# Sigmoid attention with a SiLU MLP behind it: the order of values and first products in the paired h stages, and the last set's stores

## The chip, the cores and the metric

The kernel runs on one core of one Trainium2 chip. The metric is device time in microseconds of one execution, the median of three runs. PE is the matrix engine, DVE, ACT and POOL are the vector, scalar and GpSimd engines, SP is the engine that issues most of the stores and the DMA transposes. Each engine works through its own instructions in order and waits on semaphores of the others.

## The reference

Eight batches, 12 heads, 448 positions, head size 64. Attention without a softmax, then an MLP over the 8 x 448 = 3584 rows of 768:

```python
scores = scale * np.matmul(q, k.transpose(0, 1, 3, 2)) - np.log(S)
attn = 1.0 / (1.0 + np.exp(-scores))
attn_out = np.matmul(attn, v)
...
x = attn_out.transpose(0, 2, 1, 3).reshape(B * S, H * D)
h = x @ w_in                          # 768 -> 2048
g = h * (1.0 / (1.0 + np.exp(-h)))
out = g @ w_out                       # 2048 -> 768
```

Inputs and output are float32.

## The kernel before

**Attention.** Heads are taken in quads of four; a batch has three quads (NQ), the kernel 24. `scores` (L218) makes one of a quad's seven rounds (NCH): eight matmuls of the 64*64 form into two PSUM banks (psc), then one activation on ACT into an attnT tile. `values` (L240) multiplies attnT by v: 28 matmuls of the 64*64 form, four for each round, into two banks (pav); its argument `end` stops it after so many rounds, and a later call goes on from there. After the last round DVE scales the two banks into xT (L267).

**h.** Batches 0 and 1 get their h by plain products. Batches 2 and 3, 4 and 5, 6 and 7 are taken in pairs, in three "paired h stages" (`h_pair`): a seven-product scheme over halves of w_in (wi, SI) and sums of x (tx, made on DVE by `x_sums`, L357). Each product is three matmuls of the 128*128 form with 448 columns (L378). Its first product m1 (bank pa) reads the first half of the even batch's x alone and is copied by ACT (L394); m2 adds to the same bank and SiLU on ACT writes g (gTr, L372); m5, m6, m7, m3 and m4 (banks pd, pb, pc) need the sums. The sums of the first two quads are made earlier; those of the last quad, which is the last to get its values, are made inside the stage:

```python
def last_values():
    values(g)
    after_values(g)
    for _ in x_sums(m + 1, NQ - 1, NQ):
        pass
    nc.gpsimd.tensor_copy(gate, tx[m + 1, 4][:1, NQ - 1, :1])
...
order = [(m1, 0), (m1, 1), (last_values,), (m1, 2)]
for i in range(3):
    order += [(m2, i), (silu11, i)]
order += [(m5, 0), (m6, 0), (m7, 0), (h22, 0), (m1, 3)]
```

`after_values` issues the next load of v from POOL. In the kernel before, `values(g, NCH - 1)` (L796) ahead of `h_pair` does six of the last quad's seven rounds, and `last_values` the seventh.

**PSUM banks.** Around each stage the eight banks change hands. `banks_for_h` (L78) makes a ring of them: first the two banks of the pair longest idle, then the two single banks (of the last po products), then the other pairs. `one_bank` takes them in that order, round and round.

**Output.** `sets(m)` goes through the rows of g in pairs of 128-row blocks, and `out_set` (L487) makes one pair's output by a seven-product scheme over halves of w_out; each product (po, L504) is eight matmuls of the 128*128 form with 384 columns, 0.163 us each. DVE adds them up into two output tiles osb (c11 and c12 are the halves of the first, c21 and c22 of the second). The stores are issued by SP and, at the very end, by ACT, 64 rows each (`store`, L497). In the last set of all, L514 is a copy on ACT, and the first block is stored in two halves: the left one behind L518, the right one behind L539.

The order of the whole is fixed by the program: scores and values of the next two batches are woven into the products of `sets`, then come the last products of `sets`, the paired stage, and the next `sets`. The last `sets` (from 326 us) has no attention beside it.

Of the kernel before, what the change touches and what calls it, by code (L numbers as in the profile page):

```python
# [17 lines left out]
def kernel(  # L18
# [9 lines left out]
    nc = tc.nc  # L28
# [6 lines left out]
    NCH = S // HP  # L35
# [28 lines left out]
    def banks_for_attention(doubles):  # L64
        psum.close()
        banks.clear()
        bufs_of.update(double=doubles, single=NBANK - 2 * doubles)
        for name, bufs in bufs_of.items():
            taken[name] = 0
            new_pool(name, bufs)  # L70
# [18 lines left out]
    def one_bank(name):  # L89
        if "any" in banks:  # L90
            ring.append(ring.pop(0))
            return banks["any"].tile([P, 512], F32, tag=f"any{ring[-1]}", name=name)
        taken["single"] += 1
        return banks["single"].tile([P, 512], F32, tag="single", name=name)

    def two_banks(name):
        taken["double"] += 1
        return banks["double"].tile([P, 2, 512], F32, tag="double", name=name)
# [141 lines left out]
    def values(g, end=NCH):  # L240
        b, iq = divmod(g, NQ)
        if b not in xT:
            assert b < 2 or b - 2 in h_done
            xT[b] = p2.tile([P, NPAIR, S], F16, tag="xT", name="xT")
        pav, done_rounds = part_of.pop(g, None) or (None, 0)
        if pav is None and bufs_of["double"] > 2 and "any" not in banks:
            both = two_banks("pav")
            pav = [both[:, half] for half in range(2)]
        elif pav is None:
            pav = [one_bank("pav") for _ in range(2)]  # L250
        for ch in range(done_rounds, end):
            at = attnT.pop((g, ch))
            for half in range(2):
                own = slice(half * HP, (half + 1) * HP)
                for j in range(2):
                    nc.tensor.matmul(  # L256
                        pav[half][j * D : (j + 1) * D, :S],
                        flat["v", g][own, j, ch, :],
                        at[own, j, :],
                        start=(ch == 0),  # L260
                        stop=(ch == NCH - 1),
                    )
        if end < NCH:
            part_of[g] = pav, end
            return
        for half in range(2):
            nc.vector.tensor_scalar_mul(xT[b][:, half * NQ + iq, :], pav[half][:, :S], SX)  # L267
        if iq == NQ - 1:
            ready.add(b)
# [217 lines left out]
    def out_set(a1, rows1, a2, rows2, last=False):  # L487
        lo, hi = slice(0, NHC), slice(NHC, NFC)
        osb = [p3.tile([P, DMODEL], F32, tag="osb", name="osb") for _ in range(2)]
        c11, c12 = (osb[0][:, nh * NO2 : (nh + 1) * NO2] for nh in range(2))  # L490
        c21, c22 = (osb[1][:, nh * NO2 : (nh + 1) * NO2] for nh in range(2))
        m1 = cpool.tile([P, NO2], F32, tag="m1", name="m1")
        sg = [cpool.tile([P, NHC, P], F16, tag=f"S{i}", name=f"S{i}") for i in range(1, 5)]

        def store(rows, o, cols, engines):
            for at, (row, eng) in enumerate(zip(rows, engines)):
                eng.dma_start(row[:, cols], o[at * HP : (at + 1) * HP, cols])  # L497

        left, right, whole = slice(0, NO2), slice(NO2, DMODEL), slice(0, DMODEL)

        def product(a, w):
            po = one_bank("po")
            for fc in range(NHC):
                nc.tensor.matmul(  # L504
                    po[:, :NO2], a[:, fc, :], w[:, fc, :], start=(fc == 0), stop=(fc == NHC - 1)
                )
                if fc < NHC - 1:
                    yield 163
            return po[:, :NO2]

        add, sub = nc.vector.tensor_add, nc.vector.tensor_sub
        add(sg[0], a2[:, lo], a2[:, hi])
        po = yield from product(a1[:, lo], wq[0][0])
        (act_copy if last else nc.vector.tensor_copy)(m1, po)  # L514
        sub(sg[1], sg[0], a1[:, lo])  # L515
        yield 163
        po = yield from product(a1[:, hi], wq[1][0])
        add(c11, po, m1)  # L518
        sub(sg[2], a1[:, lo], a2[:, lo])
        if last:  # L520
            store(rows1, osb[0], left, (nc.sync, nc.sync))
        yield 163
        po = yield from product(sg[1], tw[2])
        add(c12, po, m1)
        sub(sg[3], a1[:, hi], sg[1])
        yield 163
        po = yield from product(sg[2], tw[3])
        add(c22, po, c12)
        yield 163
        po = yield from product(a2[:, hi], tw[4])  # L530
        sub(c21, c22, po)
        yield 163
        po = yield from product(sg[0], tw[1])
        add(c22, po, c22)
        add(c12, po, c12)
        store(rows2, osb[1], whole, (nc.sync, nc.sync))
        yield 163
        po = yield from product(sg[3], wq[1][1])
        add(c12, po, c12)  # L539
        if last:  # L540
            store(rows1, osb[0], right, (nc.sync, nc.scalar))
        else:
            store(rows1, osb[0], whole, (nc.sync, nc.sync))
        yield 163
# [25 lines left out]
    def sets(m):  # L570
        for g in range(0, NCH - 1, 2):
            step = out_set(
                block(m, g), row_blocks(m, g), block(m, g + 1), row_blocks(m, g + 1)
            )
            for i, ns in enumerate(step):
                if m == 0 and g == 0 and i in (10, 14):
                    next(sums)
                if m == 0 and g == 0 and i in (20, 28, 36, 44):
                    next(in_sums)
                yield ns  # L580
        if m % 2 == 1:
            g = NCH - 1
            yield from out_set(
                kept, row_blocks(m - 1, g), block(m, g), row_blocks(m, g), m == B // 2 - 1
            )
# [152 lines left out]
    def burst(n, size=2):  # L738

        new = units[n : n + size]  # L740
        for u in new:
            scores(*u)
        with_values = values_if_any()
        for g, ch in new:
            if ch == NCH - 1:
                waiting.append(g)
                if 9 <= g + 3 < NQB:
                    later.extend(((g + 3, "k"), (g + 3, "q")))
        return with_values
# [15 lines left out]
    for m in range(B // 2 - 1):  # L765
        banks_for_attention(3)
        nc.scalar.activation(warm, bias_s, AF.Sigmoid)
        stream = sets(m)
        for _ in range(FIRST_DENSE):
            next(stream)  # L770

        dense = (3 + m % 2) * 7 * NHC - FIRST_DENSE - ENDING
        sizes = [2, 2, 3]
        costs = sum(SWITCH + TILE * size for size in sizes) * 2 * NQ + VALUES * (2 * NQ - 1)
        total = dense * DENSE + costs
        own = 2 * NQ * (m + 2)
        left, n = 0.0, 2 * NT_B * (m + 1)
        for size in sizes * (2 * NQ):
            left += total * size / (2 * NT_B) - SWITCH - TILE * size - VALUES * burst(n, size)
            n += size  # L780
            rows_if_any(own, nc.vector.tensor_copy)
            count = max(1, round(left / DENSE))
            left -= count * DENSE
            half = count // 2
            for i in range(count):
                next(stream)
                if i == half:
                    rows_if_any(own, nc.vector.tensor_copy)
        assert not sums_of_x
        nc.scalar.activation(warm, bias_s, AF.Silu)  # L790
        for _ in stream:
            pass
        (g,) = waiting
        waiting.clear()
        banks_for_h()
        values(g, NCH - 1)  # L796

        def last_values():
            values(g)
# [5 lines that stand above are left out]
        for i, _ in enumerate(h_pair(m + 1, last_values)):  # L805
            if i % 8 == 7:
                rows_if_any(NQB, nc.gpsimd.tensor_copy)
# [33 lines left out]
```

## Time and profile before

| | |
|---|---|
| median of 3 runs | 369.92 us (369.61 to 370.37) |
| the profiled execution | 369.69 us |
| its span, first to last instruction | 367.7 us |
| granted PE clock over the span | 0.999 of full speed |
| PE busy | 359.5 us (98%) |
| DVE, ACT, POOL busy | 251.9, 249.9, 77.8 us |
| the paired stages begin (values of the last quad) | 122.7, 212.1, 292.9 us |
| the last `sets` begins | 326.4 us |
| last matmul ends, last add ends, span ends | 363.6, 364.1, 367.7 us |

In the profile's rows, L378 is a line of the kernel, "out<-in" names the tiles, "128x448" is partitions by elements, and "xN" is the number of instructions that a row stands for. In the chain of waits a row is: start, duration, engine, tile, line, count. In the time line a row also has, in brackets, how long the engine had been idle and what ended that. In the DMA view a row has the tile, the issuing engine, the number of issues, the size of each, and the median time from issue to landing. Matmuls overlap in PE's pipeline, so a single matmul lasts longer than the distance from its start to the next one's.

### The profile page before, as it was taken

The numbers are of one execution on the slowest core, as the hardware profiler recorded it, in microseconds if no ns is written. First come the engines' busy times: TensorE is split into PE (matmuls) and PEld (weight loads), VectorE is DVE, ScalarE is ACT, GpSimd is POOL, SyncE is SP. The second block draws the span as 40 slices with busy tenths as digits, with TensorE's granted clock in tenths as the row PEclk, the third lists the DMA queues.
The fourth block names the chain that finished last, engine by engine and source line by source line (L and its number), as shares of the span: only waits on it lengthen the run. The fifth ranks groups of instructions, "written<-read, shape, count | busy, mean of one in ns | idle before, by whom it ended". The sixth has DMA issues, their size and how long they took to land. (4 is left out here: it accounts for less than half of the span.)

```text
span 367.7 us, 7596 instructions
## 1 busy us (share of the span) xinstructions
PE 359.5 (98%) x3009; PEld 183.2 (50%) x3009; DVE 251.9 (68%) x458; ACT 249.9 (68%) x339; POOL 77.8 (21%) x116
## 2 busy tenths in 40 slices
PE   7999999999999999999999999999999999999995
PEld 2554445545544555544444545554455545555553
DVE  2565569867657587867665758795756667797763
ACT  5998885479998755687777846679998856640000
POOL 8566521040060172000051047000100000000000
PEclk9999999999999999999999999999999999999999
DMA  8999999989969499007589369912863020003333
GB/s 142 200 202 202 204 204 203 187 116 141 164 100 227 110 128 180 2 0 166 92 165 206 61 128 144 128 15 51 153 111 86 21 69 0 3 0 86 87 86 86
DMA packets 65698, 42.78 MB, mean 116 GB/s; under 512 B 36096, under 2 KB 62208, under 8 KB 65664
## 3 DMA queue, kind: packets, MB, share of 16 engines
q0 software_dynamic: 27072, 22.58, 42.3%
q1 hardware_dynamic: 38240, 19.44, 26.8%
q8 instruction: 23, 0.38, 0.4%
q10 hardware_dynamic: 352, 0.30, 0.2%
q14 instruction: 11, 0.09, 0.1%
HBM read 45.61 MB, written 11.01 MB: 154 GB/s over the span
## 5 line engine op out<-in xcount | busy, mean ns | idle before, releaser
L232 ACT ACTIVATE attnT<-psc,bias_s 128x896 f16<-128x896 f32 x168 | 158.1, 1009 | 21.9 <-PE psc L225 21.6
L504 PEld LDWEIGHTS <-S 128*128 128x128 f16 x448 | 41.3, 98 | 36.5 <-issue 8.1
L225 PE MATMUL psc<-qT,kT 64*64 64x448 f16 x672 | 51.1, 362 | 1.5 <-ACT qT L186 0.6
L267 DVE TENSOR_SCALAR xT<-pav 128x448 f16<-128x448 f32 x48 | 27.7, 620 | 33.2 <-PE pav L256 33.2
L124 POOL DMA_DIRECT2D vf<-in_v_dram x24 | 17.2, 717 | 135.0 <-PE pav L256 120.9
L504 PEld LDWEIGHTS <-gTr 128*128 128x128 f16 x336 | 31.3, 98 | 26.6 <-issue 7.7
L504 PE MATMUL po<-T,S 128*128 128x384 f16 x224 | 42.0, 327 | 0.2 <-DVE S L515 0.2
L504 PE MATMUL po<-w_out_sb,gTr 128*128 128x384 f16 x224 | 41.6, 327 | 0.0
L378 PEld LDWEIGHTS <-w_in_sb 128*128 128x128 f16 x288 | 27.7, 98 | 26.9 <-issue 1.7
L504 PE MATMUL po<-w_out_sb,S 128*128 128x384 f16 x224 | 40.8, 326 | 0.0
L256 PE MATMUL pav<-attnT,vf 64*64 64x448 f16 x672 | 38.9, 350 | 0.5 <-DVE gTr L303 0.4
L288 PE MATMUL ph<-xT,w_in_sb 128*128 128x448 f16 x192 | 38.7, 353 | 0.1
L378 PE MATMUL pa<-xT,w_in_sb 128*128 128x448 f16 x144 | 33.2, 353 | 0.0
L225 PEld LDWEIGHTS <-kT 64*64 64x64 f16 x672 | 17.8, 104 | 28.8 <-issue 22.3
L378 PEld LDWEIGHTS <-SI 128*128 128x128 f16 x216 | 21.1, 98 | 20.0 <-issue 0.5
L256 PEld LDWEIGHTS <-vf 64*64 64x64 f16 x672 | 21.0, 106 | 14.0 <-issue 4.7
L288 PEld LDWEIGHTS <-w_in_sb 128*128 128x128 f16 x192 | 17.8, 98 | 19.1 <-issue 3.7
L394 ACT ACTIVATE part<-pa 128x448 f32<-128x448 f32 x24 | 13.1, 544 | 19.9 <-PE pa L378 19.0
L504 PE MATMUL po<-T,gTr 128*128 128x384 f16 x112 | 22.1, 327 | 0.0
L372 ACT ACTIVATE gTr<-pc 128x448 f16<-128x448 f32 x24 | 13.1, 544 | 12.9 <-DVE pc L388 12.5
L388 DVE TENSOR_TENSOR part<-pb,part 128x448 f32<-128x448 f32 x24 | 14.9, 621 | 8.3 <-ACT part L394 5.0
L186 ACT ACTIVATE m<-po 128x384 f32<-128x384 f32 x1 | 0.5, 491 | 27.7 <-PE po L504 27.7
(75 smaller groups left out, 467.7 us busy)
## 6 DMA issues: line engine op xcount, KB each, us to landing
out_dram<-osb SPq DMA_DIRECT2D x54, 192.0 KB, 3.0
vf<-in_v_dram POOLq DMA_DIRECT2D x24, 224.0 KB, 7.0
kf<-in_k_dram POOLq DMA_DIRECT2D x23, 224.0 KB, 7.7
qf<-in_q_dram POOLq DMA_DIRECT2D x23, 224.0 KB, 7.9
w_in_sb<-in_moe_w_in_dram POOLq DMA_DIRECT2D x16, 192.0 KB, 8.2
w_out_sb<-in_moe_w_out_dram POOLq DMA_DIRECT2D x4, 768.0 KB, 14.9
kT<-kr SPq DMA_TRANSPOSE x18, 4.1
qT<-qr SPq DMA_TRANSPOSE x18, 4.8
```

Source lines behind the costliest of these rows:

```text
L124: nc.gpsimd.dma_start(flat[name, g][:, :, c0:c1].rearrange("p i c d -> p i (c d)"), rows_in(name, g)[:, :, c0 * D : c1 * D],)
L186: nc.scalar.activation(o, i, AF.Copy)
L225: nc.tensor.matmul(psc[own, j, :S], qkT["k", g][rows, ch, own], qkT["q", g][rows, :, own], start=True, stop=True,)
L232: nc.scalar.activation(attnT[g, ch], psc[:, :, :S], AF.Sigmoid, bias=bias_s, scale=QKSCALE)
L256: nc.tensor.matmul(pav[half][j * D : (j + 1) * D, :S], flat["v", g][own, j, ch, :], at[own, j, :], start=(ch == 0), stop=(ch == NCH - 1),)
L267: nc.vector.tensor_scalar_mul(xT[b][:, half * NQ + iq, :], pav[half][:, :S], SX)
L288: nc.tensor.matmul(ph[:, :S], w_in_sb[:, cc, fc * P : (fc + 1) * P], xT[b][:, cc, :], start=(at == 0), stop=(at == NCC - 1),)
L372: nc.scalar.activation(gTr[:, r * NG + i, col + c * S : col + (c + 1) * S], h, AF.Silu, bias=0.0, scale=ISX)
L378: nc.tensor.matmul(to, w[:, n, i * P : (i + 1) * P], x[:, n], start=(start and n == 0), skip_group_check=not start, stop=(n == NQ - 1),)
L388: nc.vector.tensor_add(o, po, x)
L394: nc.scalar.activation(got[i, 1], bank[i, "a"], AF.Copy)
L504: nc.tensor.matmul(po[:, :NO2], a[:, fc, :], w[:, fc, :], start=(fc == 0), stop=(fc == NHC - 1))
```

## The change

Two edits. In the three paired h stages, the call that did six rounds of the last quad's values ahead of the first products goes; the values are then done in one piece of seven rounds by `last_values`, behind two first products (m1 of columns 0 and 1). In the last output set, the second block is stored in two halves: the left one behind L531 from SP and ACT, the right one behind L535 from SP twice.

```diff
@@ out_set
         po = yield from product(a2[:, hi], tw[4])
         sub(c21, c22, po)
+        if last:
+            store(rows2, osb[1], left, (nc.sync, nc.scalar))
         yield 163
         po = yield from product(sg[0], tw[1])
         add(c22, po, c22)
         add(c12, po, c12)
-        store(rows2, osb[1], whole, (nc.sync, nc.sync))
+        store(rows2, osb[1], right if last else whole, (nc.sync, nc.sync))
         yield 163
@@ the loop over m
         (g,) = waiting
         waiting.clear()
         banks_for_h()
-        values(g, NCH - 1)
 
         def last_values():
             values(g)
```

## The prediction

> **What bounds the kernel now.** I read the page first, then the chain of waits, then the time line of the two places that the diff touches, then the stores. The page's first part:
>
> ```profile
> span 367.7 us, 7596 instructions
> PE 359.5 (98%) x3009; PEld 183.2 (50%) x3009; DVE 251.9 (68%) x458; ACT 249.9 (68%) x339; POOL 77.8 (21%) x116
> ```
>
> PE is busy for 98% of the span, and in the view by stretches it is unbroken (32.00 of 32.00 us in 155 to 187, 27.80 of 27.80 in 218 to 245.8, 28.50 of 28.50 in 298.1 to 326.6). So a saving has to shorten PE's own stream, or what follows its last product. The chain of waits around the third paired h stage shows where the stream is not dense (start, us, what, instructions):
>
> ```profile
> 255.26 0.50 PE psc L225 x8
> 255.77 1.32 PE pav L256 x28
> ...
> 292.95 1.26 PE pav L256 x24
> 294.21 1.24 PE pa L378 x6
> 295.45 0.31 PE pav L256 x4
> 295.76 2.38 PE pa L378 x12
> 298.14 0.57 PE pd L378 x3
> ```
>
> Matmuls of the 128*128 form that follow their like take 0.57/3 = 0.189 us (the row of pd). The values (pav) are of the 64*64 form, four of them side by side: the 28 that follow psc, of the same form, take 1.32 us, seven rounds of 0.189. The four rows at 292.95 to 298.14 last 5.19 us, while seven rounds and 18 products would be 25 x 0.189 = 4.73. The rest, 0.46 us, lies at the four changes of form, about 0.115 each: 1.26 against 1.13 for six rounds, 1.24 against 1.13, 0.31 against 0.19, 2.38 against 2.27. The first two stages have the same four rows (1.26, 1.24, 0.31, 2.38 from 212.13). The other two views are the time line of the same place and of the end:
>
> ```profile
> 292.98 0.56 DVE L539 TENSOR_TENSOR osb<-po,osb 128x384 f32<-128x384 f32 x1 [0.28 <-PE po L504]
> 295.80 1.16 DVE L267 TENSOR_SCALAR xT<-pav 128x448 f16<-128x448 f32 x2 [2.25 <-PE pav L256]
> 296.87 0.38 DVE L357 TENSOR_TENSOR tx<-xT 128x448 f16<-128x448 f16 x1
> 297.97 0.73 PE L378 MATMUL pd<-tx,SI 128*128 128x448 f16 x3
> ```
> ```profile
> 360.98 0.55 DVE L531 TENSOR_TENSOR osb<-osb,po 128x384 f32<-128x384 f32 x1 [0.74 <-PE po L504]
> 362.28 0.56 DVE L534 TENSOR_TENSOR osb<-po,osb 128x384 f32<-128x384 f32 x1 [0.75 <-PE po L504]
> 362.87 1.77 SPq L497 DMA_DIRECT2D out_dram<-osb  x3
> 363.58 0.56 DVE L539 TENSOR_TENSOR osb<-po,osb 128x384 f32<-128x384 f32 x1 [0.28 <-PE po L504]
> 364.17 0.55 ACTq L497 DMA_DIRECT2D out_dram<-osb  x1
> ```
>
> The first says how much time the sums of x have before PE asks for them; the second, that the end is one add (363.58 to 364.14), one pair of stores at 364.17 and their landing.
>
> **Part one, the values in one piece.** Removed is the call that puts six rounds ahead of the first two products; the seventh round's call now issues all seven. No instruction is added or lost: 28 pav and 18 pa matmuls stay, in the order 6 pa, 28 pav, 12 pa instead of 24, 6, 4, 12. The po products ahead are of pa's form (pd to po at 245.77 goes on without a gap), so the changes go from four to two: po to pav and pav to pa before the last round fall away. That is 2 x 0.115 = 0.23 us in each of three stages, 0.69 us, all on PE's stream.
>
> What covers it: the first product takes the first two banks of the ring, those that pav took at 292.95 without a wait, so it has them. The values now take the two single banks of the last po products. One is freed by L535, the other by L539, which ends at 293.54; the values begin after six products, near 292.95 + 1.13 = 294.08, so 0.5 us to spare. The fourth m1 now gets the bank of the first m1, not one of pav's. The first activation of gTr (L372, three from 297.04, 1.68 us) has read it by about 297.6, and that m1 starts at 299.68: 2 us to spare. Last round to xT to sums: the last round of values starts two changes earlier too, so L267, the sums and their first reader all move by about 0.23. Of the three matmuls of pd only the third needs the new third of tx, at 297.97 + 2 x 0.189 = 298.35, against 297.25 when the first sum ends: 1.1 us to spare, as before. ACT's copies of m1 come earlier and ACT is free at 293.28, after its table load and the one small activation behind it. The load of v that POOL issues behind these values keeps its place in POOL's queue and its wait for the same matmuls. Nothing is moved past anything on DVE, ACT, SP or POOL. Bounds for the part: 0.72 (if the smaller changes are as dear as the largest, 6 x 0.12), and 0 if another engine sets the end of a later stage; I take 0.69, since PE never stands idle for another engine by more than 0.2 us between 128 and 326 (one wait for DVE S L515, itself behind PE's own values).
>
> **Part two, the last set's second block.** Its left half goes to SP and ACT behind the sub at L531, at about 361.57 in the old clock, and the two stores behind L535 shrink from 192 to 96 KB each. Two DMA issues are added. SP's is 0.5 us long (three take 1.77 us) and SP otherwise stands waiting for the add; ACT's takes 0.55 and ACT has nothing between its copy at 355.60 and its last store at 364.17. Behind SP's issue stand the right halves, which wait for 362.84 anyway. The add at L534 reads and writes only the right half; the same arrangement for the first block (left stored at 357.55, next add into its right half at 358.20, long before the store has landed) runs without a wait. So the cost on the way is nothing. The gain: the last stores now find 192 KB less ahead of them. The rows, by the issues in the DMA view:
>
> ```profile
> out_dram<-osb SPq DMA_DIRECT2D x2, 96.0 KB, 2.1
> ...
> out_dram<-osb SPq DMA_DIRECT2D x2, 192.0 KB, 2.7
> ...
> out_dram<-osb SPq DMA_DIRECT2D x1, 96.0 KB, 2.4
> out_dram<-osb ACTq DMA_DIRECT2D x1, 96.0 KB, 2.6
> ```
>
> In order: left halves of the first block with nothing around them, the whole rows, and the last two. The last, 2.6, sets the end: 364.17 + 2.6 = 366.8, and 0.9 us of closing follow up to 367.7. Bounds: 0, if ACT's store is late for a reason of its own (at the start of the program ACT's store takes 3.3 us against SP's 3.1, issued in the same moment, though it is the smaller one), and 2.6 - 2.1 = 0.5. Keeping ACT 0.2 behind SP and SP at 2.1 gives 2.3, a gain of 0.3; two right halves are still in flight when the last pair is issued, so I take 0.2. In the rows the fixed parts of stores overlap: the last four were issued within 1.3 us and took 2.4 to 2.7 each, so two more issues need not cost two more landings. The Trainium skill, page "DMA: Bandwidth & Descriptors", section "Bandwidth", speaks against this part: it wants transfers of 1 MiB or more, and by that a halved store only repeats its fixed cost and this part would give 0.
>
> **Sum.** 0.69 + 0.20 = 0.89 us. The profiled execution took 369.69 (span 367.7 and 2.0 around it), 0.23 under the median of the three runs, so it becomes 368.80, and the median 369.92 becomes 369.03.
>
> **Rivals.** *The stores give nothing*: the last pair lands 2.6 after issue whatever went ahead. Then only 0.69 is left: 369.23. For it: the smaller load at the start, late on ACT too. Against it: SP's half took 2.4 with the whole rows ahead and 2.1 without. *The stores give more*: both land in 2.1, 0.5 saved, 1.19 in all: 368.73. *The earlier stream runs into something with a clock of its own* in a later stage, most likely the transposes and loads between 128 and 245, where the page's DMA digits are at 9 (128 to 147 and 220 to 239): what the first two stages saved is waited away and 0.23 + 0.20 is left, 369.5. Against it, the keys are fetched and transposed three quads ahead. *Slower*: the add at L534 has to wait until the left half is out, because the store reads the tile that it writes. It would start not at 362.28 but when the halves issued at 361.57 have landed, after 2.1 to 2.6, at 363.7 to 364.2; L535, L539 and the last stores follow it, 1.4 to 1.9 later, and with 0.69 saved the kernel ends 0.7 to 1.2 later, about 370.9. It decides only if dependence is kept by tile and not by columns; the first block's left store, issued at 357.55 ahead of the add at 358.20, speaks against it.
>
> **Chances.** Forecast 0.54, stores nothing 0.18, stores more 0.10, waited away 0.11, slower 0.07. About 0.2% (0.74 us) is what a measurement of this kernel can tell from no change, so faster means under 369.18 and slower over 370.66. The three runs shown lie 0.3 below to 0.45 above their median; a new median may be 0.2 off. With that, the forecast falls under 369.18 in about 8 of 10, stores nothing in 4 of 10, stores more always, the others never: 0.43 + 0.07 + 0.10, about 0.61. Slower 0.06, the rest 0.33. The range leaves out slower and some of the scatter: 368.5 (stores more, a little low) to 369.8 (waited away, a little high).
>
> **What would show it.** Right: in the chain behind the last po of each set, pa x6 of 1.13, pav x28 near 1.44, pa x12 near 2.38, pd at most 4.97 us after the last po instead of 5.19; in the end stretch, L531 to L539 at the same distances as now, 96 KB rows only, and the last store landing 2.3 to 2.5 after its issue. Wrong: idle PE ahead of the third pd matmul (the sums), ahead of pav (the bank that L539 frees) or ahead of psc (keys); a gap of over 2 us between L531 and L534; or a last store that still takes 2.6.

## The result and the profile after

The changed kernel takes 369.53 us (median of 20 runs, 368.83 to 369.92), the kernel before 370.12 us in 20 runs beside it (369.30 to 370.37). The ratio is 0.9984, 95% interval 0.9977 to 0.9990: 0.59 us faster, between 0.37 and 0.85. The forecast was 0.89 faster; the time lies in the range, and the gain falls short of the 0.2% that the forecast set for "faster".

The chain of waits of the changed kernel around the third paired stage (start, us, engine, tile, line, count):

```profile
289.92 2.96 PE po L504 x18
292.87 1.13 PE pa L378 x6
294.01 1.45 PE pav L256 x28
295.46 2.38 PE pa L378 x12
297.83 0.57 PE pd L378 x3
```

From the end of po to pd are now 4.96 us where there were 5.19. The six products behind po take 1.13, that is 6 x 0.189 with nothing added, since po and pa have the same form; 28 values take 7 x 0.189 + 0.13, the next products 12 x 0.189 + 0.11. Two surcharges are left of four. From the last po matmul's start to the first pd matmul's the records have 5.353, 5.353 and 5.352 us before and 5.122 three times after: 0.23 us in each stage, 0.69 in all.

The time line of the same place shows that nothing took their room:

```profile
292.91 0.56 DVE L541 TENSOR_TENSOR osb<-po,osb 128x384 f32<-128x384 f32 x1 [0.28 <-PE po L504]
295.49 1.16 DVE L267 TENSOR_SCALAR xT<-pav 128x448 f16<-128x448 f32 x2 [2.02 <-PE pav L256]
296.56 0.38 DVE L357 TENSOR_TENSOR tx<-xT 128x448 f16<-128x448 f16 x1
```

The add that frees the values' second bank (L539 before, L541 now) ends at 293.47 and the first value starts at 293.94. The first sum ends at 296.94, and the third pd matmul, which reads it, starts at 298.05.

The end, in the time line and then in the DMA view of the last pair:

```profile
361.98 0.56 DVE L536 TENSOR_TENSOR osb<-po,osb 128x384 f32<-128x384 f32 x1 [0.75 <-PE po L504]
362.56 1.77 SPq L497 DMA_DIRECT2D out_dram<-osb  x3
363.28 0.56 DVE L541 TENSOR_TENSOR osb<-po,osb 128x384 f32<-128x384 f32 x1 [0.28 <-PE po L504]
363.87 0.50 ACTq L497 DMA_DIRECT2D out_dram<-osb  x1
```
```profile
out_dram<-osb SPq DMA_DIRECT2D x1, 96.0 KB, 2.1
out_dram<-osb ACTq DMA_DIRECT2D x1, 96.0 KB, 2.4
```

The add into the right half (L534 before, L536 now) starts 0.72 us after the left half's issue at 361.26, long before that has landed, with the same 0.75 of idle time as before. The last pair lands in 2.1 and 2.4 us where it took 2.4 and 2.6. And yet from the end of the last add to the end of the span are now 3.74 us where there were 3.59. What has grown lies behind the landing: 1.34 us from the last landing (366.24) to the end, against 0.97 (from 366.76). SP's waits in the last eight microseconds, of before and then of after (who waited for what: us in total, times, longest), and its closing semaphore instructions from the last landing on (count, shortest/median/longest in ns), again before and then after:

```profile
SPq L836 <- DMA out_dram<-osb: 1.7, 3, 0.6
...
SPq L837 <- DMA out_dram<-osb: 1.8, 1, 1.8
```
```profile
L836 SPq EVENT_SEMAPHORE  x4: 17/22/28, 366.8 to 367.7; - x4
...
L837 SPq EVENT_SEMAPHORE  x10: 17/28/28, 366.3 to 367.5; - x10
```

SP ends the program by going through a fixed row of waits, one for each of eight completion semaphores that the transfers issued by SP and ACT take in turn; one wait follows the other at 0.06 us. Before, SP got through four of them at once, stood three times as the last four stores landed, and had four instructions left when the last was down: the last two waits of the row and two of the end that all engines share. After, it stood once, 1.8 us at the head of the row, and had ten left, all eight of the row and the same two. In the records the last pair has the semaphores 117 and 118 before, the last two of the row, and 107 and 109 after, the first two: two more transfers have moved it round by two places. Six more waits of 0.06 are 0.37 us, more than the 0.22 by which the landing came forward.

The two profiled executions differ by only 0.15 us in span. PE's stream from the first scores on gave 0.71 (0.69 of it in the three stretches) and the end took 0.15, but 0.41 was lost before the first change is reached: the first scores start at 7.00 us instead of 6.60. That stretch is the same code in both kernels and is taken up at the end.

### The profile page after: what moved, and what is told of

Same layout as the page of the kernel before. It is cut to its first block, busy times and chain, and to the rows that moved or that the text cites. A ratio compares the mean times of both kernels' runs of the same rounds, so it can differ in the third digit from the quotient of the medians.

```text
span 367.6 us, 7594 instructions
## 1 busy us (share of the span) xinstructions
PE 359.3 (98%) x3009; PEld 183.8 (50%) x3009; DVE 251.8 (69%) x458; ACT 250.0 (68%) x339; POOL 77.5 (21%) x116
```

## The experiments

The theory (A): a change of form on PE costs 0.115 us, the paired edit saves two in each stage, and the store edit gives 0.2 at the landing and loses 0.37 in the closing row. The rival (B): the paired edit is worth only what the whole change gave, the stores nothing, and the longer closing is chance. All kernels with a ratio ran against the kernel before on the same chip.

**The first edit alone.** Only the call `values(g, NCH - 1)` is taken out.

```diff
         banks_for_h()
-        values(g, NCH - 1)
```

> The first edit alone: the values of the last quad in one piece behind two first products, the stores as before. Theory A (two changes of form fewer on PE are worth 0.23 us in each of three stages, and the store edit of the whole change costs more than it gives): 0.70 us faster than before, a ratio of 0.9981, so a little faster than the whole change; PE's stream after the third stage 0.70 ahead once the opening is taken off; closing as before, last store landing 2.6 us after its issue, 0.93 from its landing to the end. Theory B (the paired part is worth only the 0.59 us of the whole change, the stores nothing): ratio 0.9984.

Ratio 0.9985 (0.9976 to 0.9993), 0.55 us. The interval holds both theories' numbers. The records decide: 5.122 us in each stage, and from the last product ahead of the first stage to the last matmul 0.70 saved (240.75 us before, 240.05 now); last store 2.57 after its issue, closing 0.97. In span this execution is only 0.06 us shorter than that of the kernel before, since it lost 0.66 ahead of the first stage, in code that both kernels share: 0.46 up to the first scores (at 7.06) and 0.2 between these and the first stage. So counted from the first scores the stream is 0.51 ahead, not the 0.70 that was expected.

**The second edit alone.** In the changed kernel the call of values is put back; the halved store stays.

```diff
         banks_for_h()
+        values(g, NCH - 1)
```

> The second edit alone: the last set's second block stored in two halves, the values as before. Theory A (the last stores land 0.2 us sooner, but two more DMA issues put their completion at the head of the row of waits that SP goes through at the end, so that six more of these, 0.06 us each, come after the landing): 0.1 to 0.2 us slower than before, ratio 1.0004; last store lands 2.4 after its issue, and 1.3 us instead of 0.93 pass from there to the end. Theory B (the stores give and cost nothing): ratio 1.0000, 0.93 from landing to end.

Ratio 1.0001 (0.9992 to 1.0009): too near for the times to tell. The records agree with A: landing 2.38, closing 1.35, and 3.76 us from the last add to the end against 3.59, a loss of 0.17. SP's waits have the one long stand:

```profile
SPq L838 <- DMA out_dram<-osb: 1.8, 1, 1.8
```

**Six more issues on top of the whole change**, so that there are eight more than before and the semaphores come round.

```diff
-        store(rows2, osb[1], right if last else whole, (nc.sync, nc.sync))
+        for cols in (left, right) if 2 in halved else (right if last else whole,):
+            store(rows2, osb[1], cols, (nc.sync, nc.sync))
...
+            for cols in (left, right) if 1 in halved else (whole,):
+                store(rows1, osb[0], cols, (nc.sync, nc.sync))
...
+    HALVED = {(3, 0): (1, 2), (3, 2): (2,)}
```

> The whole change, and three earlier stores of the last group of sets also in halves: six more DMA issues, eight more than before, so that the last stores stand at the end of SP's closing row of waits again. Theory A: closing after the last landing back from 1.3 to 0.93 us, the landing 2.4 after issue: 0.92 us faster than before, ratio 0.9975, some 0.35 faster than the whole change. Theory B (the longer closing is chance, or belongs to the halves): like the whole change, ratio 0.9984, or slower by what six more issues cost.

369.10 us against 369.99, ratio 0.9977 (0.9968 to 0.9986): the fastest median of the whole case together with the fifth kernel below. The landing keeps its 2.37 and the closing is back at 0.99, so that 3.40 us pass from the last add to the end: 0.34 less than in the changed kernel, 0.19 less than before.

```profile
SPq L842 <- DMA out_dram<-osb: 1.5, 2, 0.9
...
L842 SPq EVENT_SEMAPHORE  x4: 17/22/28, 366.1 to 367.0; - x4
```

Four instructions are left after the landing, as before. The interval overlaps that of the whole change, so the step of 0.34 is shown by the records and only supported by the times.

**Two more issues and nothing else**, with the stores at the end and the values as before; one earlier store is halved by the same `halved` argument as in the run above.

```diff
+    HALVED = {(3, 0): (2,)}
```

> The kernel before with one earlier store of the last group of sets in halves: two more DMA issues some 28 us ahead of the end, nothing else. Theory A: the last store lands 2.6 after its issue as before, but its completion stands at the head of the closing row: 1.3 us from landing to end, 0.37 us slower than before, ratio 1.0010. Theory B: no change, 0.93 from landing to end.

Ratio 1.0008 (0.9999 to 1.0017), 370.45 us; the interval just reaches 1. One store was halved 28 us ahead of the end, and 3.98 us pass from the last add to the end instead of 3.59: landing 2.61, closing 1.34.

```profile
SPq L841 <- DMA out_dram<-osb: 2.1, 1, 2.1
...
L841 SPq EVENT_SEMAPHORE  x10: 17/28/28, 366.7 to 367.9; - x10
```

This is the change's hidden cost by itself, without a gain: 0.39 us. Rival B falls with it. The closing is no chance either: it is 0.97 to 0.99 us in all five profiled executions in which the last pair has the last two places of the row, and 1.34 to 1.35 in all three in which it has the first two.

**All values first.** The seven rounds go ahead of the first products, which are not moved ahead.

```diff
-        values(g, NCH - 1)
+        values(g)
+        after_values(g)
...
         def last_values():
-            values(g)
-            after_values(g)
             for _ in x_sums(m + 1, NQ - 1, NQ):
```

> The kernel before with all seven rounds of the last quad's values ahead of the first products, so two changes of form as in the changed kernel, but the products not moved ahead. Theory A (the number of changes of form on PE sets the gain): 5.12 us from the last po product's last matmul to the first pd matmul instead of 5.35, 0.70 us faster than before, ratio 0.9981, the same as the first edit alone. Theory B (the gain comes from doing two products ahead of the values): 5.35 us and no change.

The chain around the third stage:

```profile
289.96 2.96 PE po L504 x18
292.92 1.45 PE pav L256 x28
294.37 3.51 PE pa L378 x18
297.88 0.57 PE pd L378 x3
```

Again 4.96 us, and 5.12 from the last po matmul to pd in the three stages. Ratio 0.9974 (0.9963 to 0.9984); its lower time than the first edit alone, with which it shares every measured stretch, is within the two intervals. It is the count of changes that saves, not which work goes first.

**Values in three pieces**, six changes of form.

```diff
-        values(g, NCH - 1)
+        values(g, 3)
+
+        def more_values():
+            values(g, NCH - 1)
...
-        order = [(m1, 0), (m1, 1), (last_values,), (m1, 2)]
+        order = [(m1, 0), (more_values,), (m1, 1), (last_values,), (m1, 2)]
```

> The kernel before with the last quad's values in three pieces (3 rounds, m1 of column 0, 3 rounds, m1 of column 1, 1 round): six changes of form instead of four. Theory A: 5.58 us from the last po matmul to the first pd matmul, 0.70 us slower than before, ratio 1.0019. Theory B: no change, since no product goes ahead of the values.

```profile
293.85 0.69 PE pav L256 x12
294.54 0.67 PE pa L378 x3
295.21 0.69 PE pav L256 x12
295.90 0.68 PE pa L378 x3
296.58 0.31 PE pav L256 x4
```

Each piece carries its own surcharge: 0.69 against 3 x 0.189 = 0.57, 0.67 against 0.57, 0.31 against 0.19. In the records 5.58 us from po to pd, and the ratio is 1.0021 (1.0012 to 1.0029), 0.8 us slower. With two, four and six changes the stretch is 5.12, 5.35 and 5.58: a line of 0.115 a change. The Trainium skill, page "TensorEngine Tiling (Array Packing)", section "Tiling Modes", says that changing the tiling mode, not just the tile, drains the engine; it gives no price, and these three runs give one. They show the price and not what PE does in it.

**Four more issues**, in a single run (370.51 us), so that only its profile is read.

```diff
+    HALVED = {(3, 0): (1, 2)}
```

> The kernel before with two earlier stores in halves: four more DMA issues. Theory A (each issue moves the last stores along SP's closing row of eight waits, in a circle): four waits of 0.06 us behind the landing more than before, 0.97 + 0.25 = 1.22 us from landing to end, between the 0.97 of before and the 1.34 that two more issues gave. Theory B (more issues make the closing longer in proportion): 1.7 us; (only the first two matter): 1.34.

```profile
SPq L841 <- DMA out_dram<-osb: 2.0, 3, 0.8
...
L841 SPq EVENT_SEMAPHORE  x8: 17/28/28, 367.3 to 368.5; - x8
```

The closing takes 1.23 us, with eight instructions left after the landing. With 0, 2, 4 and 8 more issues it takes 0.97, 1.34, 1.23 and 0.99: a circle of eight places, not a price for each issue.

## Why the prediction was right and where it was off

**Values in one piece: right.** Foretold were 0.69 us from two changes of 0.115 fewer in each of three stages, and 5.35 became 5.12 in each. The covers named for it held with the room that was foretold: 0.47 us at the bank that the last add frees (0.5 was said), 1.1 us at the sums. The saving reached the end of PE's stream in full: between the opening and the last matmul the changed kernel is 0.71 shorter (356.62 and 355.91 us). The rival by which a later stage waits the saving away did not come (from the first pd matmul of a stage to the last po matmul ahead of the next, 83.98 and 75.47 us pass before, 83.97 and 75.47 after); neither did the one by which the add into the right half has to wait for the left half's store.

**Landing: right in size.** Between 0 and 0.5, the forecast took 0.2 for the earlier landing of the last pair; it was 0.22 (2.59 to 2.37), and 0.21 with the second edit alone. ACT's store still lands behind SP's, by 0.24 us where it was 0.21, both issued in the same moment. It is the halved last block that moves the landing: 2.37, 2.38 and 2.37 us in the three kernels that have it, 2.57 to 2.62 in the six that do not, those with two and four more issues among them. That the bytes ahead are what counts, as the forecast has it, fits and was not tested apart. The rule of the Trainium skill that transfers should be large ("DMA: Bandwidth & Descriptors", "Bandwidth") does not decide here: SP's right halves land in 2.1 us where the whole rows took 2.7, and at the very end only the last landing counts.

**Closing: the step that failed.** "Two DMA issues are added ... So the cost on the way is nothing", and "0.9 us of closing follow up to 367.7". The issues were priced on the queues of SP and ACT, where they cost nothing, and the closing was carried over as a constant. It isn't one: it depends on the place of the last landing in SP's row of waits, and the two issues moved that from the last place to the first. So the term for the stores, +0.20 of gain, was in truth 0.22 gained less 0.37 lost, -0.15. The sum is then 0.69 - 0.15 = 0.54 us, which lies within the interval of the measured 0.59 (0.37 to 0.85); the forecast's 0.89 lies outside it. That the time is in the forecast's range all the same is no merit of this term, which had the wrong sign: it is small beside the first, and the range was kept wide for the rivals. Two of these, "the stores give nothing" (0.69 us) and "waited away" (0.43), lie nearer to 0.54 than the forecast, each for a reason that the runs do not bear out: the landing did improve, and nothing was waited away.

**The threshold.** With the closing priced, the forecast would have been 0.54 us or 0.15%, less than the 0.2% from which it called a change faster.

**Small slips.** Four of them change nothing in the sum. The transfers at the start of the program that the forecast calls stores are loads of q. Its chain of waits begins at 187.75 us and so shows the second and third stage, not the first; the records have 5.353 us there too. Its upper bound of 0.72 takes 0.12 for the dearest change, for which its own row gives 0.13 (1.26 against 1.13). And 0.43 + 0.07 + 0.10 is 0.60, not 0.61.

## What to carry to other kernels

A change of matmul form is a cost that no idle time shows: PE counts as busy for 5.10 of 5.10 us in each of the first two stages before. It is read by dividing a run's length by its count and comparing with the dense rate. So work of one form belongs in one piece, and here it mattered little where. An edit that adds transfers near the end is to be priced to the last instruction of the program, not to the last landing: compare the closing rows of the two profiles, and if more waits are left after the last landing than before, the number of transfers ahead of it can put it back, as six more issues did here. A gain of 0.2% in a kernel whose opening varies by as much is better read from stretches within the trace than from medians of a few runs.

## What the runs showed of the hardware that was not expected

The opening varies from execution to execution. The first scores of the profiled executions start between 6.09 and 7.06 us after the span's start, in code that all kernels share. The time line of the first transposes, of the kernel before and then of the changed one, shows one source:

```profile
5.30 0.41 PE L196 MATMUL ptrq<-ident,qf 128*64 128x128 f16 x8
...
5.41 0.64 PE L196 MATMUL ptrq<-ident,qf 128*64 128x128 f16 x8
```

The same eight matmuls take 0.41 and 0.64 us; in the records their pairs follow each other at 56 ns from 5.38 on in the first execution, and at 107 ns until 6.16 in the second. The view by stretches has a granted clock of 1.00 there in both, so that only the pace shows it. The Trainium skill, page "TensorE: Matmul & The Clock Gate", "Part 1: The HAM clock gate", says that PE runs at half its rate until it has been busy for about 3.4 us, that the window runs freely, and that the moment therefore varies from run to run; it gives 106.7 and 55.6 ns for matmuls of 128 columns, and the paces here agree. The 3.4 us do not hold here as a fixed time: the first matmul starts at 1.46 us in all nine executions, and the faster pace comes between 2.5 and 2.8 us later with the second edit alone, but more than 4.8 us later in four others.

The first scores follow this moment. The pace changes between 4.0 and 4.3 us with the second edit alone, between 4.84 and 5.16 with two more issues, between 4.85 and 5.30 before, at 5.8 with six more issues, at 6.2 in the changed kernel and after 6.27 in the other four; the first scores start at 6.09, 6.45, 6.60, 6.87, 7.00 and four times near 7.06 us, in the same order as far as the moments can be told apart. That the one sets the other is read from this order; no run varied it by itself. On the way to the first stage the spread shrinks from 0.97 to 0.79 us (the last po matmul ahead of it starts between 122.34 and 123.13). Loads land a little earlier or later too (SP's first one 3.1 and 3.2 us after its issue); what share of the scatter they have was not measured apart.
